# Memory products of three late batches behind U of the next batch's first step, in free columns of banks d and b; two softmax steps later

## The chip, the cores and the metric

The kernel runs on one core of one Trainium2 chip. The metric is device microseconds of one execution, lower is better. TensorE (PE in the profile) multiplies matrices into PSUM, which has eight banks of 512 fp32 columns; VectorE (DVE) and ScalarE (ACT) read PSUM and work on tiles in SBUF; SyncE (SP) issues most transfers. Each engine takes its instructions in order.

## The reference

Eight batches of eight heads, 576 positions each, head width 64, 32 memory slots per head. Then a gated layer over all 4608 rows of width 512, inner width 1536. Everything is fp32.

```python
a = exp(phi - max(phi));  a = a / (sum(a) + 1e-9)           # softmax over the memory slots
k_m = einsum('bhsm,bhsd->bhmd', a, k)                       # memory: keys and values of 32 slots
v_m = einsum('bhsm,bhsd->bhmd', a, v)
attn = softmax(q @ k_m.T / 8);  o = attn @ v_m
x = o rearranged to (4608, 512)
out = (sigmoid(x @ w_gate) * (x @ w_val)) @ w_out
```

## The kernel before

**Precision.** An fp32 product is made of three faster matmuls of a high and a low part (`_hi`, `_lo`): high by high, high by low, low by high. ScalarE rounds the high part, VectorE subtracts it from the whole (`rest`, L185). The memory products are plain fp32.

**Stages.** Batches 0 to 2 and the conversions of the weights lie in an early part, to some 287 us. The late part treats batches 3 to 7 (QUAD is 3) in 12 steps each, f = 0 to 11, one per 128 columns of the inner width. The attention's probabilities of the batch (`at`) are multiplied by U, which is v_m times the weights of two steps: in every even step `pair_u` makes the U of the next two steps in 16 fp32 matmuls (rows 64x512) into banks c and a, with weights that the transfer `ring<-wgv` has brought. A step (class `Group`) then forms its gate and value tiles by seven products p(1) to p(7) of sums of the operands, three matmuls of 128x288 each, and four out tiles of three matmuls 128x512 (`acc`). `add`, `gate`, `product_of`, `to_hi`, `to_lo` are the work on VectorE and ScalarE between a step's products and its out tiles; a step's out tiles run during the next step. In the program g is the group of this step and h the one before.

**Banks.** Four banks serve the late products: a, c, and two that change places, d in even steps and b in odd ones. Products 1, 6, 7 and 4 go into d (or b), 2 into a, 5 and 3 into c. A step's tile in d or b takes columns 0 to 287; the rest of that bank (`beside`) is free and takes the scores of the next batch in steps 2, 4, 6. Product 7 of h comes at the head of the next step, product 4 and 6 later in it: add 3 of h reads h's bank after product 7, and product 4 of h adds onto it after that.

**Order.** The order of the late loop is written out by hand; other work is hung into it at named places by `side(place)`, from a plan that `late_sides(b)` makes. In the program's order the places of a step are: "u" (behind pair_u), "m", "m3", out tiles, product 2, product 5, "E", copy p5, "act1", "B", product 4 of h, product 6, copy x, "x", "act2", out tile, "m2", product 3, "end", add 1, "B2", "act3", out tile, "Z", "load".

**Memory.** `memory(n)` is a generator whose pieces `go` calls: four transposes of the weights a and copies, then the memory products of a batch, 80 matmuls of 128 columns into 32 rows each, 40 for each half g of the heads (`kvm0` or `kvm1`, and `kvt` with `tails` for the last 64 positions), then their scaling by 1/sum (`rz`, L445 on ScalarE), four transposes of what that leaves (`row`), and copies to `kT` and `vT`. For batches 5, 6 and 7 (n > QUAD + 1) the products and the scaling lie in step f = 11 of batch n - 2, place "m", in bank a, and the transposes and copies in f = 0 of batch n - 1. The softmax of phi for those batches begins with `a_max` (L375). When a batch's memory products are done, SP may load the next batch's keys and values into the same tiles (`load_next`).

**Closing.** The two sigmoids (`gate`) of a step go at its end, or, when `close` is set, at the head of the next step behind copy s1.

Of the kernel before, what the change touches and what calls it, by code (L numbers as in the profile page):

```python
# [17 lines left out]
P = 128  # L18
B, H, S, D, M = 8, 8, 576, 64, 32
DM, DFF = 512, 1536  # L20
NG = 2
NKT = 4
NFT = DFF // P
SF = 4
# [16 lines left out]
QUAD = 3  # L41
# [63 lines left out]
def attn_moe_kernel(  # L105
# [27 lines left out]
    def bank():  # L133
        if "banks" in pools:
            return late_bank("a")
        name = next(turn_of) if spread else None
        if name is None:
            return pu.tile([P, 512], F32, name="pu_t")
        return po.tile([P, 512], F32, name=name)

    def att(shape, name, bufs=1):
        return sb.tile(shape, F32, name=name, bufs=bufs)
# [46 lines left out]
    def in_turn(do, *args, **kw):  # L189


        with ExitStack() as behind:
            if last_pe[0] is not None:
                behind.enter_context(tc.issue_after(last_pe[0].ins))
            last_pe[0] = do(*args, **kw)  # L195

    def matmul(*args, **kw):
        in_turn(nc.tensor.matmul, *args, **kw)

    def transpose(*args, **kw):  # L200
        in_turn(nc.tensor.transpose, *args, **kw)
# [196 lines left out]
    def memory(b):  # L398


        ph = loaded[b, "phi"]
        pf = ph.rearrange("p g s -> p (g s)")
        in_rows = b < QUAD or "banks" in pools
        if in_rows:
            am = [mb.tile([P, DM], F32, name="row", bufs=4) for _ in range(NG)]
            am = [t.rearrange("p (c x) -> p c x", c=SF) for t in am]
        else:
            am = att([P, 2 * S], "e")[:, : NG * SF * P]
            am = [a.rearrange("p (c x) -> p c x", c=SF) for a in (am[:, : SF * P], am[:, SF * P :])]
        for g in range(NG):  # L410
            pt = bank().rearrange("p (c x) -> p c x", c=SF)
            for c in range(SF):
                o = (g * (SF + 1) + c) * P
                transpose(pt[:, c, :], pf[:, o : o + P], ident)
            yield
            nc.scalar.copy(am[g], pt)
            yield
        pt = bank()
        transpose(pt[:, :P], pf[:, SF * P : (SF + 1) * P], ident)
        yield  # L420
        for g in range(NG):
            gs = slice(g * TAIL, (g + 1) * TAIL)
            nc.scalar.copy(tails[gs, g, :], pt[gs, :P])
        yield
        km = loaded[b, "kv"]
        kvp = bank().rearrange("p (g w d) -> p g w d", g=4, w=2)
        for g in range(NG):
            for c in range(SF + 1):
                for h in range(4):
                    hs = slice(h * M, (h + 1) * M)  # L430
                    xs = slice(h * P, (h + 1) * P)
                    if c < SF:
                        l, r = am[g][:, c, hs], km[g][:, c, xs]
                    else:
                        l, r = tails[:, g, hs], km["tail"][:, xs]
                    matmul(kvp[hs, g], l, r, start=(c == 0), stop=(c == SF))
            if g or b < QUAD:
                yield
        if in_rows:
            kb = mb.tile([P, DM], F32, name="row", bufs=4)  # L440
        else:
            kb = att([P, 2 * S], "e")[:, : NG * 4 * D]
        kb = kb.rearrange("p (g w j d) -> p g w j d", g=NG, w=2, j=2)
        for g in range(NG):
            nc.scalar.activation(  # L445
                kb[:, g],
                kvp[:, g].unsqueeze(2).broadcast_to([P, 2, 2, D]),
                AF.Copy,
                scale=loaded[b, "rz"][:, g : g + 1],
            )  # L450
        yield
        kvT = bank().rearrange("p (w g x) -> p w g x", w=2, g=NG)
        for g in range(NG):
            for w in range(2):
                transpose(kvT[:, w, g, :], kb[:, g, w].rearrange("p j d -> p (j d)"), ident)
        yield
        kvTs[b] = [keep.tile([P, NG, P], F32, name=f"{w}T", bufs=5 if w == "v" else 1) for w in "kv"]
        for w in range(2):
            nc.scalar.copy(kvTs[b][w], kvT[:, w])
            yield  # L460
# [54 lines left out]
    def s_max(b, c=None):  # L515

        e = blocks(b, c)
        w = e.shape[2]
        mx = att([P, 2, S // 32], "mx")[:, :, :w]
        nc.vector.tensor_reduce(mx, e, axis=AX.X, op=ALU.max)  # L520
        yield
        nc.vector.tensor_tensor(
            e, e, mx.unsqueeze(3).broadcast_to([P, 2, w, M]), op=ALU.subtract
        )
        yield
# [345 lines left out]
    def step(do, *args, **kw):  # L871
        with queued():
            return do(*args, **kw)
# [24 lines left out]
    now = [None, None]  # L898
# [257 lines left out]
    def late_bank(name):  # L1156
        return pools["banks"].tile([P, 512], F32, name=name)
# [72 lines left out]
    for i, (b, f, at_start, at_end) in enumerate(steps[:MAIN]):  # L1230
# [9 lines left out]
        if i in KEEP_W:  # L1240
            k = KEEP_W[i]
            w, kept_k = wg[:, 2 * k : 2 * k + 2], kept_w[k].rearrange("p (f k n) -> p f k n", f=2, k=NKT)
            move(kept_k[D:], w[D:])
            move(kept_k[:D, :, :, :P], w[:D, :, :, :P])
            for j in range(2):
                t = mb.tile([P, DM], F32, name="row", bufs=4)[:D]
                t = t.rearrange("p (k n) -> p k n", k=NKT)
# [86 lines left out]
    def late_sides(b):  # L1334

        n, m = b + 1, b + 2
        plan = {}

        def put(f, place, do, *args):
            plan.setdefault((f, place), []).append((do, args))  # L1340

        def go(x, k=1):
            for _ in range(k):
                next(memories[x])

        if n < B:
            if n > QUAD + 1:
                put(0, "m2", go, n)
                put(0, "end", go, n, 2)
            soft = [s_max(n, c) for c in range(len(ROOMFULS))]  # L1350
            norm = normalize(n)
            for c in range(len(ROOMFULS)):
                put(2 * c + 2, "u", scores, n, c)
                put(2 * c + 2, "m3", to_blocks, n, c)
                put(2 * c + 2, "Z", next, soft[c])
                put(2 * c + 3, "B", next, soft[c])
            put(6, "act3", s_exp, n, slice(0, 2 * ROOM))
            put(7, "act3", s_exp, n, 2)
            put(8, "E", next, norm)
            put(8, "Z", next, norm)  # L1360
            if m == B:
                put(9, "E", next, norm)
            put(9, "Z", cross, n)
            put(10, "B", sums_at, n, 1, 2)
            put(10, "act2", at_hi, n, "b11")
            put(10, "Z", at_lo, n, "b11")
            put(11, "m", at_hi, n, "b21")
            put(11, "E", sums_at, n, 3, 4)
            put(11, "B", at_lo, n, "b21")
            put(11, "x", at_hi, n, "t1")  # L1370
            put(11, "B2", at_lo, n, "t1")
            put(11, "act2" if m < B else "x", at_hi, n, "t2")
            put(11, "Z", at_lo, n, "t2")
        if b > QUAD:
            put(0, "act", at_hi, b, "b22")
            put(0, "act", at_hi, b, "t3")
            put(0, "E", at_lo, b, "b22")
            put(0, "B", at_lo, b, "t3")
            put(0, "act2", at_hi, b, "t4")
            put(0, "B2", at_lo, b, "t4")  # L1380
        if m < B:
            def begin_m():
                memories[m] = memory(m)

            put(2, "B", a_max, m)
            put(7, "act1", a_exp, m, (0,))
            put(7, "act2", a_exp, m, (1,))
            put(7, "Z", a_sum, m)
            put(7, "Z", begin_m)
            for f, place in ((8, "m2"), (9, "m"), (10, "m2"), (11, "m")):  # L1390
                put(f, place, go, m)
                put(f, "end" if place == "m2" else "m", go, m)
            if m + 1 < B:
                put(11, "Z", load_next, m + 1)
        if b + 1 < B:
            put(0, "load", load_q, b + 1)
        return plan
# [15 lines left out]
    for b, f in [(b, f) for b in range(QUAD, B) for f in range(NFT)]:  # L1413
        if f == 0:
            plan = late_sides(b)
# [5 lines left out]
        n = (b - QUAD) * NP + f // 2  # L1421
        odd = f % 2
        more = n + 1 < NPAIRS
        g = Group(b, f)
# [5 lines left out]
        if h:  # L1430
            step(h.add, 3)
        step(g.copy, "s1")
        if f in (2, 4, 6) and b + 1 < B:
            if b == QUAD and f == 2:
                step(part_hi, n, "s")
                step(later_lo)
            step(part_lo, n, "s")
            while gates:
                step(*gates.pop(0))
# [85 lines left out]
            step(h.to_lo)  # L1525
        side("B2")
        gates.extend([(g.gate, 0), (g.gate, 1)])
        close = f in (1, 3, 5) and b + 1 < B
        while gates and not close and not (f == 7 and b + 1 < B):
            step(*gates.pop(0))  # L1530
        side("act3")
# [85 lines left out]
```

## Time and profile before

| | |
|---|---|
| three runs | 714.0, 714.28 and 714.55 us, median 714.28 |
| the profiled execution | 713.97 us, its span 712.2 us |
| PE busy | 702.7 us, 99% of the span |
| VectorE busy | 554.1 us, 78% |
| ScalarE busy | 444.2 us, 62% |
| granted clock of TensorE | full speed in all 40 slices, mean 0.998 |

The span is what the profiler saw from the first to the last instruction; the time of the execution has 1.77 us more. Matmuls overlap in the records: rows of one product start 0.13 to 0.23 us apart and each lasts longer. The late part, in which the change lies, is 12 steps for each batch from 287 us on; f = 11 of batch 4 ends and f = 0 of batch 5 begins around 368 us.

### The profile page before, as it was taken

The page shows a single profiled execution, that of the slowest core. Times are in us where ns is not written, and L with a number is a line of the kernel's source. Part 1 is how long each engine was busy: PE and PEld are TensorE (multiplying, and loading weights), DVE is VectorE, ACT ScalarE, POOL GpSimd, SP SyncE. Part 2 cuts the span into 40 slices and gives each one's busy share as a digit, 9 for nine tenths or more (in the row PEclk, how much of TensorE's full clock was granted, in tenths as well). Part 3 has the DMA queues.
Part 4 walks back from the last instruction along what each step waited for, and adds up shares of the span by engine and source line. Part 5 has one row for each costly group of instructions (what it writes and reads, how often), then busy time and mean ns, then how long its engine had stood idle before and what let it go on. Part 6 is the DMA issues. An engine that isn't in the chain of part 4 may idle for free.

```text
span 712.2 us, 14476 instructions
## 1 busy us (share of the span) xinstructions
PE 702.7 (99%) x5623; PEld 580.2 (81%) x5623; DVE 554.1 (78%) x1108; ACT 444.2 (62%) x1033; POOL 27.9 (4%) x55
## 2 busy tenths in 40 slices
PE   8899999999999999999999999999999999999997
PEld 6666898888988888878888888888888888788886
DVE  4999998688787675588888779787797778977663
ACT  4765667544355454557877577865877667686553
POOL 0000110111100110100000000000000000000000
PEclk9999999999999999999999999999999999999999
DMA  8966768779986545641175113652213422151102
GB/s 341 410 236 247 319 191 321 284 245 278 301 241 230 185 147 199 228 143 66 60 269 201 60 61 118 228 183 82 108 64 134 159 71 75 61 175 63 61 1 74
DMA packets 36084, 123.22 MB, mean 173 GB/s; under 512 B 3952, under 2 KB 11376, under 8 KB 28848
## 3 DMA queue, kind: packets, MB, share of 16 engines
q1 hardware_dynamic: 31296, 106.71, 42.7%
q0 software_dynamic: 4560, 15.47, 6.1%
q8 instruction: 44, 0.72, 0.4%
q14 instruction: 24, 0.20, 0.1%
q10 hardware_dynamic: 160, 0.13, 0.1%
HBM read 96.73 MB, written 25.56 MB: 172 GB/s over the span
## 4 chain that ended last, share of the span: by engine, by line
PE 92%; DVE 4%; DMA 2%; ACT 1%; issue 1%; SPq 0%; DVEq 0%; ACTq 0%
PE acc L195 38%; PE pu_t L195 21%; PE c L195 11%; PE a L195 8%; PE b L195 7%; PE d L195 7%; DMA q<-in_qT_dram 1%; DMA ph<-in_phiT_dram 1%; DVE wg L286 0%; DVE nmx L375 0%; DVE e L513 0%; DVE u_lo L185 0%; DVE row L772 0%; ACT ph L170 0%; DVE left L286 0%
## 5 line engine op out<-in xcount | busy, mean ns | idle before, releaser
L195 PE MATMUL acc<-wo_hi,g_hi 128*128 128x512 f32 x372 | 151.4, 407 | 0.0
L195 PE MATMUL acc<-wo_hi,g_lo 128*128 128x512 f32 x372 | 147.1, 395 | 0.4 <-DVE g_lo L185 0.4
L195 PE MATMUL acc<-wo_lo,g_hi 128*128 128x512 f32 x372 | 146.5, 394 | 0.0
L195 PE MATMUL pu_t<-at,u_hi 128*128 128x320 f32 (+1 forms) x560 | 116.5, 304 | 0.8 <-DVE at L185 0.8
L195 PEld LDWEIGHTS pu_t<-at,u_hi 128*128 128x128 f32 x560 | 92.1, 188 | 8.7 <-issue 1.9
L195 PEld LDWEIGHTS acc<-wo_hi,g_hi 128*128 128x128 f32 x372 | 69.8, 188 | 29.6 <-issue 10.6
L195 PEld LDWEIGHTS acc<-wo_hi,g_lo 128*128 128x128 f32 x372 | 69.8, 188 | 18.1 <-DVE g_lo L185 1.1
L195 PE MATMUL pu_t<-at,u_lo 128*128 128x256 f32 (+1 forms) x264 | 77.5, 294 | 0.0
L195 PEld LDWEIGHTS acc<-wo_lo,g_hi 128*128 128x128 f32 x372 | 70.0, 188 | 5.4
L1198 ACT COPY c_p<-c 128x288 f32<-128x288 f32 x60 | 24.0, 399 | 61.3 <-PE c L195 60.6
L170 ACT ACTIVATE sg<-pu_t 128x256 f32<-128x256 f32 (+1 forms) x70 | 28.6, 412 | 48.3 <-PE pu_t L195 40.9
L1202 DVE TENSOR_TENSOR z<-a,c_s 128x288 f32<-128x288 f32 x60 | 27.1, 452 | 32.0 <-PE a L195 31.9
L722 ACT CAST g_hi<-sg 128x256 fp32r<-128x256 f32 x66 | 26.4, 406 | 38.2 <-DVE sg L712 37.2
L712 DVE TENSOR_TENSOR sg<-pu_t,sg 128x320 f32<-128x320 f32 (+1 forms) x69 | 30.9, 453 | 24.1 <-ACT sg L170 14.0
L195 PEld LDWEIGHTS pu_t<-at,u_lo 128*128 128x128 f32 x264 | 49.6, 188 | 0.0
L170 ACT ACTIVATE z<-z 128x288 f32<-128x288 f32 x120 | 47.9, 442 | 1.5 <-DVE z L1202 0.8
L1214 ACT CAST g_hi<-z 128x512 fp32r<-128x512 f32 x60 | 37.4, 623 | 17.9 <-DVE z L1209 17.8
L1202 DVE TENSOR_TENSOR z<-c,c_x 128x288 f32<-128x288 f32 x60 | 27.3, 455 | 27.3 <-PE c L195 24.5
L185 DVE TENSOR_TENSOR g_lo<-z,g_hi 128x512 fp32r<-128x512 f32 x60 | 41.0, 684 | 2.3 <-ACT g_hi L1214 2.3
L195 PE MATMUL a<-ring,vT 64*32 64x512 f32 x232 | 31.4, 601 | 0.0
L195 PE MATMUL c<-ring,vT 64*32 64x512 f32 x232 | 31.4, 601 | 0.0
L1209 DVE TENSOR_TENSOR z<-z 128x288 f32<-128x288 f32 x60 | 27.0, 450 | 5.4 <-ACT z L170 0.7
(242 smaller groups left out, 1631.3 us busy)
## 6 DMA issues: line engine op xcount, KB each, us to landing
ring<-wgv SPq DMA_DIRECT2D x30, 1024.0 KB, 4.9
kvm<-in_kvm_dram SPq DMA_DIRECT2D x14, 1024.0 KB, 8.6
at<-at SPq DMA_DIRECT2D x18, 576.0 KB, 7.5
q<-in_qT_dram SPq DMA_DIRECT2D x16, 512.0 KB, 5.2
part<-row POOLq DMA_DIRECT2D x24, 256.0 KB, 5.6
row<-part SPq DMA_DIRECT2D x24, 256.0 KB, 4.0
words<-in_wo_dram SPq DMA_DIRECT2D x8, 512.0 KB, 8.3
words<-in_wgv_dram SPq DMA_DIRECT2D x4, 1024.0 KB, 5.9
```

The costliest lines, as they stand in the source:

```text
L170: last_act[0] = nc.scalar.activation(*args, **kw)
L185: return nc.vector.tensor_tensor(lo, x, hi.bitcast(F32), op=ALU.subtract)
L195: last_pe[0] = do(*args, **kw)
L712: last_prod[0] = nc.vector.tensor_tensor(prod, ps[1][:, :n], sg[:, :n], op=ALU.mult)
L722: nc.scalar.copy(hi, prod[:, : 2 * P])
L1198: copy(getattr(self, name), self.c if name == "p5" else self.d)
L1202: nc.vector.tensor_tensor(self.z[:, i], x, y, op=ALU.add)
L1209: nc.vector.tensor_tensor(self.z[:, 2 + i], x, self.z[:, i], op=ALU.mult)
L1214: nc.scalar.copy(self.g[0], self.z[:, 2:4, : 2 * P])
```

## The change

Four things. First, for batches 5, 6 and 7 (`aside`) the memory products go from f = 11, "m", to the next batch's f = 0, "u", that is behind pair_u. They don't go into bank a but into columns 288 and up of banks that steps hold: half 0 into the bank of h (b, from f = 11), half 1 into that of g (d), without clearing the bank at the start. Their scaling goes to f = 0, "act1". Second, `close` is set in f = 11 too. Third, `a_max` of batch 5 goes from f = 2 of batch 3 to f = 4. Fourth, in batch 6 the last batch's `cross` (the transpose of probabilities, L969) goes from f = 9, "Z", to f = 10, "m3", and two of its sums from "B" to "B2".

```diff
+        aside = b > QUAD + 1
+        kvp = [unit.beside[:, :P] for unit in now] if aside else bank().rearrange("p (g x) -> p g x", g=4)
+        kvp = [kvp[g] if aside else kvp[:, g] for g in range(NG)]
...
-                    matmul(kvp[hs, g], l, r, start=(c == 0), stop=(c == SF))
+                    matmul(
+                        kvp[g][hs], l, r, start=c == 0 and not aside, stop=c == SF, skip_group_check=aside,
+                    )
...
             if n > QUAD + 1:
+                put(0, "u", go, n)
+                put(0, "act1", go, n)
                 put(0, "m2", go, n)
                 put(0, "end", go, n, 2)
...
-            put(9, "Z", cross, n)
-            put(10, "B", sums_at, n, 1, 2)
+            put(*((9, "Z") if m < B else (10, "m3")), cross, n)
+            put(10, "B" if m < B else "B2", sums_at, n, 1, 2)
...
-            put(2, "B", a_max, m)
+            put(4 if b == QUAD else 2, "B", a_max, m)
...
-            for f, place in ((8, "m2"), (9, "m"), (10, "m2"), (11, "m")):
+            for f, place in ((8, "m2"), (9, "m"), (10, "m2")):
...
-        if f in (2, 4, 6) and b + 1 < B:
+        if f in (2, 4, 6) and b + 1 < B or f == 0 and QUAD < b < B - 1:
...
-        close = f in (1, 3, 5) and b + 1 < B
+        close = f in (1, 3, 5) and b + 1 < B or f == NFT - 1 and b + 2 < B
```

On PE, in f = 0 of batch 5, the memory products (`b<-kvm0`, `d<-kvm1`, and `kvt` with `tails`) stand in the changed order behind the last matmul of U (`a<-ring`):

```order
L195 MATMUL a_4568<-ring_4417,vT_3544 32x512
L195 MATMUL b_4485<-kvm0_3589,row_4303 32x128 [waits DVE_49]
L195 MATMUL b_4485<-kvm0_3589,row_4303 32x128 x15
L195 MATMUL b_4485<-kvt_3587,tails_83 32x128 x4
L195 MATMUL d_4558<-kvm1_3591,row_4304 32x128 [waits Activation_49]
L195 MATMUL d_4558<-kvm1_3591,row_4304 32x128 x15
L195 MATMUL d_4558<-kvt_3587,tails_83 32x128 x4
L195 MATMUL acc0_3775<-wo2_hi_2397,g2_hi_4524 128x512
```

Before, the first out tile (`acc0`) came there, and the memory products stood in f = 11 in bank a; the wait for DVE in the second row is for add 3 of h (`z<-b,c_p5`), which reads bank b.

On PE in the same step, from product 5 (`c`) through product 4 of h (`b`) to product 6 (`d`), first of the kernel before:

```order
L195 MATMUL c_4644<-at_3317,s_lo_4416 128x288 [waits DVE_49]
L195 MATMUL b_4485<-at_3319,u_hi_4252 128x288 [waits DVE_49]
L195 MATMUL b_4485<-at_3320,u_hi_4252 128x288
L195 MATMUL b_4485<-at_3319,u_lo_4253 128x288
L195 MATMUL d_4605<-at_3319,s_hi_4415 128x288
```

and of the change:

```order
L195 MATMUL c_4640<-at_3317,s_lo_4416 128x288 [waits DVE_49]
L195 MATMUL b_4485<-at_3319,u_hi_4252 128x288 [waits Activation_49]
L195 MATMUL b_4485<-at_3320,u_hi_4252 128x288
L195 MATMUL b_4485<-at_3319,u_lo_4253 128x288
L195 MATMUL d_4558<-at_3319,s_hi_4415 128x288 [waits Activation_49]
```

The matmuls stand as they stood; the first of product 4 and the first of product 6 wait for ScalarE, where product 4 waited for VectorE and product 6 for nothing.

On ScalarE in the same step, from the casts of the probabilities (`at`) through the copies of product 5 and of bank d (`c_p5`, `c_x`), first of the kernel before:

```order
L1000 CAST at_3319<-q_4390 128x288
L1000 CAST at_3317<-q_4390 128x288
L1198 COPY c_p5_4599<-c_4644 128x288 [waits PE_49,Activation_49]
L1198 COPY c_x_4600<-d_4605 128x288 [waits DVE_49,PE_49]
L1214 CAST g2_hi_4660<-z_4481 128x512 [waits DVE_49]
```

and of the change:

```order
L1005 CAST at_3317<-q_4390 128x288
L1203 COPY c_p5_4552<-c_4640 128x288 [waits PE_49,Activation_49]
L450 ACTIVATE row_4647<-b_4485,rz_4226 128x256 [waits DMASW7_49,DMAHW1_49,DMASW1_49,DVE_49]
L450 ACTIVATE row_4647<-d_4558,rz_4226 128x256
L1203 COPY c_x_4553<-d_4558 128x288 [waits PE_49]
```

The two scalings of the memory (`row<-b,rz` and `row<-d,rz`) stand between the two copies; before they stood in f = 11 and read bank a.

## Rows read from the trace of the kernel before

**Rows 1.** The page: busy us, share of the span and instructions of each engine.

```profile
PE 702.7 (99%) x5623; PEld 580.2 (81%) x5623; DVE 554.1 (78%) x1108; ACT 444.2 (62%) x1033; POOL 27.9 (4%) x55
```

**Rows 2.** Timeline, PE in f = 11 of batch 4: start, us, engine, line, operation, out<-in.

```profile
360.81 0.43 PE L195 MATMUL b<-at,u_hi 128*128 128x288 f32 x2
...
361.30 1.08 PE L195 MATMUL a<-kvm,row 128*32 128x128 f32 x32
...
363.62 0.50 PE L195 MATMUL acc<-wo_hi,g_hi 128*128 128x512 f32 x1
...
363.96 0.39 PE L195 MATMUL acc<-wo_lo,g_hi 128*128 128x512 f32 x1
```

**Rows 3.** Timeline, PE in f = 0 of batch 5.

```profile
369.82 0.59 PE L195 MATMUL c<-ring,vT 64*32 64x512 f32 x1
...
370.39 0.50 PE L195 MATMUL acc<-wo_hi,g_hi 128*128 128x512 f32 x1
...
372.29 0.42 PE L195 MATMUL c<-at,s_hi 128*128 128x288 f32 x2
...
372.69 0.42 PE L195 MATMUL b<-at,u_hi 128*128 128x288 f32 x2
```

**Rows 4.** Timeline, DVE from f = 11 to f = 0 there.

```profile
365.77 0.46 DVE L1202 TENSOR_TENSOR z<-a,c_s 128x288 f32<-128x288 f32 x1 [1.75 <-PE a L195]
...
367.11 0.45 DVE L1209 TENSOR_TENSOR z<-d,z 128x288 f32<-128x288 f32 x1
...
370.35 0.45 DVE L185 TENSOR_TENSOR at<-q,at 128x288 fp32r<-128x288 f32 x1
...
370.72 0.45 DVE L1202 TENSOR_TENSOR z<-b,c_p 128x288 f32<-128x288 f32 x1
```

**Rows 5.** Timeline, DVE in f = 11 of batch 6, which has no memory products.

```profile
620.13 0.45 DVE L1209 TENSOR_TENSOR z<-d,z 128x288 f32<-128x288 f32 x1
...
621.27 0.69 DVE L185 TENSOR_TENSOR g_lo<-z,g_hi 128x512 fp32r<-128x512 f32 x1 [0.32 <-ACT g_hi L1214]
...
621.88 0.45 DVE L185 TENSOR_TENSOR at<-q,at 128x288 fp32r<-128x288 f32 x1
```

**Rows 6.** Timeline, ACT from f = 11 to f = 0 of batch 5.

```profile
363.76 0.84 ACT L445 ACTIVATE row<-a,rz 128x256 f32<-128x256 f32 x2 [0.83 <-PE a L195]
...
372.94 0.40 ACT L1198 COPY c_p<-c 128x288 f32<-128x288 f32 x1 [0.64 <-PE c L195]
```

**Rows 7.** Line 445, late batches: shortest, median and longest in ns, first and last start.

```profile
L445 ACT ACTIVATE row<-a,rz x6: 466/472/476, 363.8 to 534.2; 128x256 f32<-128x256 f32 x6
```

**Rows 8.** Timeline, PE and DVE in f = 2 of batch 3.

```profile
305.14 0.43 PE L195 MATMUL c<-at,u_hi 128*128 128x288 f32 x2
...
306.57 1.34 DVE L375 TENSOR_REDUCE nmx<-ph 128x2 f32<-128x1152 f32 x1
...
310.09 0.50 PE L195 MATMUL acc<-wo_hi,g_lo 128*128 128x512 f32 x1 [0.36 <-DVE g_lo L185]
...
310.82 0.42 PE L195 MATMUL c<-at,u_hi 128*128 128x288 f32 x2
```

**Rows 9.** Timeline, PE and DVE in f = 2 of batch 4.

```profile
385.43 0.42 PE L195 MATMUL c<-at,u_hi 128*128 128x288 f32 x2
...
386.00 1.34 DVE L375 TENSOR_REDUCE nmx<-ph 128x2 f32<-128x1152 f32 x1
...
390.28 0.42 PE L195 MATMUL c<-at,u_hi 128*128 128x288 f32 x2
```

**Rows 10.** Timeline, PE in f = 10 of batch 6.

```profile
611.59 0.43 PE L195 MATMUL c<-at,u_hi 128*128 128x288 f32 x2
...
616.69 0.43 PE L195 MATMUL c<-at,u_hi 128*128 128x288 f32 x2
```

**Rows 11.** DMA issues from 360 to 384 us: KB each, median us from issue to landing.

```profile
kvm<-in_kvm_dram SPq DMA_DIRECT2D x2, 1024.0 KB, 6.6
```

**Rows 12.** Timeline, PE: U of f = 2 in batch 5.

```profile
382.14 0.61 PE L195 MATMUL c<-ring,vT 64*32 64x512 f32 x1
```

More of the change, by code (lines that the diff above doesn't have):

```diff
@@ L425, in memory @@
         km = loaded[b, "kv"]
-        kvp = bank().rearrange("p (g w d) -> p g w d", g=4, w=2)
+        aside = b > QUAD + 1
+        kvp = [unit.beside[:, :P] for unit in now] if aside else bank().rearrange("p (g x) -> p g x", g=4)
+        kvp = [kvp[g] if aside else kvp[:, g] for g in range(NG)]
+        kvp = [t.rearrange("p (w d) -> p w d", w=2) for t in kvp]
         for g in range(NG):
@@ L446, in memory @@
                 kb[:, g],
-                kvp[:, g].unsqueeze(2).broadcast_to([P, 2, 2, D]),
+                kvp[g].unsqueeze(2).broadcast_to([P, 2, 2, D]),
                 AF.Copy,
```

## Prediction

> **What bounds the kernel now.** I read the page's busy shares first: TensorE (PE in the rows) is at work for 702.7 of the span's 712.2 us [rows 1], and its granted clock is at full speed in all 40 slices. So a microsecond comes off only where PE has less to issue or stops waiting, and a microsecond goes on wherever PE is made to wait; ScalarE (ACT) and VectorE (DVE) count only where PE stands in line behind them. Next I read the timeline of the two steps that the change touches, f = 11 of batch 4 and f = 0 of batch 5 (batches 6 and 7 repeat it). In f = 11 the memory products lie between product 1 and the out tiles without a hole [rows 2], and in f = 0 PE goes from U to the out tiles and from product 5 to product 4 without one [rows 3]. In these two steps there is thus no stall to win; what the change can bring there is the small cost of switching shapes, and what it can lose is a new wait.
>
> **The move of the memory products.** The matmuls stay the same, 80 of them (40 per half). *Taken out of f = 11:* product 1 starts at 360.81 and a product occupies PE for 0.40 (372.29 to 372.69 in rows 3), so the first out matmul could start at 361.21; it starts at 363.62, and it is 0.50 long where the next is 0.39 [rows 2]. That is 2.41 + 0.11 = 2.52 us out. *Put into f = 0:* from the first memory product to the out tile it is 363.62 - 361.30 = 2.32 [rows 2]; the step from U's second half to what follows, 370.39 - 369.82 = 0.57 [rows 3], is paid already, with whichever block follows. So -0.2 per batch. I keep 0 and -0.35 as bounds, since no row shows this block right behind U.
>
> **First new wait: half 0 behind add 3.** In the changed order half 0 is written into bank b (the first order fence), and PE waits there for DVE: b still holds product 7 of the step before, which add 3 reads. When does add 3 end? Measure all on the old time axis, with PE 2.52 earlier after f = 11's place "m". Half 0 would be due at 369.82 - 2.52 + 0.57 = 367.87. On DVE, add 0 now idles 1.75 for PE [rows 4]; that idle goes, but no more than that, for DVE itself is full from there on. So the product with gate 0 starts at 367.11 - 1.75 = 365.36. From it to the g_lo of the same step it is 621.27 - 620.13 = 1.14 where DVE runs without PE's memory block, and 0.61 from g_lo to the next remainder [rows 5]; two more starts at 0.37 (370.35 to 370.72) and add 3's own 0.45 follow [rows 4]. That is 365.36 + 1.14 + 0.61 + 0.37 + 0.37 + 0.45 = 368.30, or some 368.25 if DVE catches up its little. PE waits from 367.87 to there: **+0.4** per batch, bounds 0.2 and 0.55. Behind the waiting matmul on PE stand both halves, the out tiles, and products 2 and 5. Half 1 goes into bank d and waits for ACT's copy of that bank; the copy needs product 1 alone, which lies ahead of U, and is done before half 0 is.
>
> **Second new wait: product 4 behind the scale.** Product 4 accumulates into bank b's first 288 columns, and half 0 now lies in b's other columns until ACT has scaled it. In the second order fence product 4 waits for ACT where it waited for DVE before; the third shows where the scale stands on ACT: right behind the copy of product 5. But product 5 is the product directly before product 4 on PE. So PE must finish 5, ACT must copy it, then scale half 0, and only then may 4 start. With S the start of product 5: the copy starts at S + 0.65 (372.94 - 372.29) and lasts 0.40 [rows 3, 6]. A scale lasts 0.472 [rows 7], and two of them 0.84 together [rows 6], so neighbours on ACT overlap by 0.10. The scale of half 0 ends at S + 0.65 + 0.40 - 0.10 + 0.47 = S + 1.42; product 4 started at S + 0.40 before [rows 3]. That is 1.02 later; with a first matmul 0.11 slower after the hole, as behind the memory block [rows 2], it is **+1.1** per batch, bounds 0.9 and 1.2. Nothing covers it: between 5 and 4 the list gives PE no other work. Product 6 then needs the scale of half 1, which ends 0.37 after the first; 6 stands 0.40 behind 4, so it waits for nothing more. Behind 4 everything moves along: the product with gate 1, g_hi, g_lo, the transposes of the scaled memory (these get more room, the scale being earlier beside them), and the next step.
>
> The Trainium skill, *PSUM — Partial Sum Buffer*, section "PSUM bank collisions raise a hardware error", says that no two engines may access one bank within the same 32 partitions at the same time, disjoint columns included, and that software must put a dependency there. This speaks against the change: columns that are free are not a bank that is free. By that page the two waits stand, as in the sum; were columns independent, the sum would lose them, which is the second rival. No row of before shows two engines inside one late bank at a time, and none shows the contrary.
>
> Per batch: -0.2 + 0.4 + 1.1 = +1.3; three batches **+3.9** (bounds 2.3 and 5.2, from the ends of all three at once).
>
> **The maximum.** In batch 3's f = 2 the reduction of 1.34 us stands in DVE's line, g_lo comes late, and the third out matmul waits 0.36 for it [rows 8]. The step from product 5 to product 5 is 310.82 - 305.14 = 5.68; the same step of batch 4, also with a reduction in it, has 390.28 - 385.43 = 4.85 and no stall [rows 8, 9]. So **-0.83** when it leaves f = 2. At f = 4 it meets a step like batch 4's and costs 0 by that row; the upper bound is what it cost before, 0.83.
>
> **The turned probabilities (batch 6).** The transpose, in f = 9's place "Z", makes DVE late in f = 10: that step is 616.69 - 611.59 = 5.10 [rows 10] where 4.85 is the clean length [rows 9], so at most -0.25. One step later, DVE has the same work to do before f = 11's products: **-0.1**, bounds -0.25 and 0.
>
> **Closing the gates later** (ACT's two sigmoids and a DVE remainder move from the end of f = 11 into f = 0): ACT idled 0.64 before its copy of product 5 [rows 6], and the memory products put 2.32 more between; two sigmoids over as many columns as that copy (0.40) fit in that. 0.
>
> **Loads.** The loads for the next batch's keys and values now wait for the later products, and the ring load for U of f = 2 stands behind them on SP. One of the two large ones takes 6.6 us to land [rows 11], the ring load is as large as one, and the three stand one behind the other: 9.9 in all if the two large ones shared those 6.6 us, 13.2 if not; I take the middle, 11.6. Room, from the end of the products (370.39 on the old axis) to U of f = 2 at 382.14 [rows 3, 12]: 11.75, and the second wait adds 1.1. So 0, and up to 1 per batch, in two batches only, since for batch 7 nothing is loaded.
>
> Sum: 3.9 - 0.83 - 0.1 = +2.95 us (rounded 3.0). The profiled execution took 713.97, its span 712.2, with 1.77 outside; the new span comes to 715.15 and this execution to 716.9. The median of the three runs is 714.28, 0.31 above the profiled one; on it the forecast is **717.2 us**.
>
> **Rivals.** *A load is late* (chance 0.09): the chain of loads overruns its room by 0.5 in two batches, 717.2 + 1.0 = 718.2. For it: room and length are nearly equal. Against: the wait for the scale lengthens the room. *The first wait isn't there* (0.12): DVE catches up in f = 11, where nothing else holds it, and PE waits for the scale alone: 717.2 - 1.2 = 716.0. For it: 0.4 is a small difference of two long chains. Against: DVE's work there is counted from rows. *The bank waits cost nothing* (0.06), the other side: the scale of half 0 is over when product 4 comes up, because ACT gets to it early, or columns of a bank stand alone. Then 3 x -0.2 - 0.83 - 0.1 = -1.5, 712.8 us. It decides when the waits are under 0.5 per batch in sum, at which the time is that of before ((0.83 + 0.1) / 3 + 0.2). For it: the products of all other rows in f = 0 lose nothing. Against: on ACT's list the scale stands behind a copy that cannot start before product 5 ends, and PE has nothing in between.
>
> **How the numbers follow.** The forecast has 0.73, with its own range 716.3 to 718.0 (each term about half of the way to its bound, three times over). The range 715.6 to 718.3 takes in the one-wait case with its spread and the late load's middle; left out are the case without waits and the worst of the loads. A difference of 0.2%, 1.43 us, is about what a measurement of this kernel can tell from no change. Faster by that means under 712.85: two thirds of the last rival, 0.04. Within it, up to 715.71: the rest of it and the low tail of the one-wait case, 0.08. Slower: 0.88.
>
> **What would show it.** In the changed profile product 4 of f = 0 in batches 5 to 7 should begin some 1.45 after product 5, with an idle time put down to ACT's scale; the first memory product some 0.4 late, put down to DVE's add 3; out tiles of f = 11 directly behind product 1; batch 3's f = 2 in 4.85. The prediction is wrong if product 4 follows product 5 at 0.40, if the first out matmul after f = 0's U is not displaced by more than 2.4, or if U of f = 2 waits for its ring load.

## The result, and the profile after

| | median | lowest to highest | runs |
|---|---|---|---|
| before | 714.18 us | 713.97 to 714.55 | 6 |
| changed | 719.01 us | 717.18 to 720.21 | 6 |

The ratio is 1.0064, with a 95% interval of 1.0054 to 1.0074: the change costs 4.6 us, or 0.6% (the two medians themselves are 4.8 apart). The forecast was 717.2, its range ended at 718.3. The direction was right, the size too small. The changed kernel's six runs differ by 3 us and the six of before by 0.6; over the 27 runs of before that went with later experiments it was 2.9 too (713.68 to 716.61), so the spread alone says little.

Batches are counted below as the late loop counts them (its `b`). Counted so, the rows from 360 to 373 us are f = 11 of batch 3 and f = 0 of batch 4: two steps after product 5 at 372.29 [rows 3] comes f = 2 of batch 4 at 385.43 [rows 9]. The headings of [rows 2], [rows 3], [rows 4], [rows 6] and [rows 12], the text on the site around 368 us and the prediction put them one batch too high; [rows 5] and [rows 8] to [rows 10] are counted right. The three sites of the move are f = 11 of batches 3, 4 and 5, each with f = 0 of the next batch. No sum changes by this.

The profiled execution is the slowest of the six, 720.21 us with a span of 718.4 (before 713.97 and 712.2), so it shows the loss at its largest. The page's shares hardly move (compare [rows 1]); the view of what waits for what, PE's rows, says more. Its columns are the engine, tile and line that waited, what for, us in total, times, and the longest:

```profile
PE b L195 <- ACT row L450: 2.8, 3, 0.9
PE b L195 <- DMA q<-in_qT_dram: 2.7, 2, 2.0
...
PE b L195 <- DVE z L1207: 0.9, 3, 0.3
```

None of the three rows has a counterpart in the kernel before. The first and the third are the two bank waits of the forecast, three times each. The second, scores waiting for a load of q, isn't in it.

PE in the timeline of the changed kernel, from f = 11 of batch 3 into f = 0 of batch 4 (rows 2 and 3 are the same places before):

```profile
359.96 0.29 PE L195 MATMUL b<-at,u_lo 128*128 128x288 f32 x1
...
360.09 0.40 PE L195 MATMUL acc<-wo_hi,g_hi 128*128 128x512 f32 x1
...
366.20 0.59 PE L195 MATMUL c<-ring,vT 64*32 64x512 f32 x1
...
367.14 1.08 PE L195 MATMUL b<-kvm,row 128*32 128x128 f32 x32 [0.30 <-DVE z L1207]
...
369.46 0.50 PE L195 MATMUL acc<-wo_hi,g_hi 128*128 128x512 f32 x1
...
371.36 0.43 PE L195 MATMUL c<-at,s_hi 128*128 128x288 f32 x2
...
372.84 0.53 PE L195 MATMUL b<-at,u_hi 128*128 128x288 f32 x2 [0.92 <-ACT row L450]
```

The out tile of f = 11 now follows product 1 at once. From U's second half to the memory products it is 0.94, where 0.57 stood ahead of the out tile [rows 3]: 0.37 for add 3. The block itself takes 2.32 as before, and product 4 starts 1.48 after product 5, which was 0.40.

What they wait for, on DVE and ACT of the same execution:

```profile
364.15 0.45 DVE L1214 TENSOR_TENSOR z<-d,z 128x288 f32<-128x288 f32 x1
...
365.29 0.69 DVE L185 TENSOR_TENSOR g_lo<-z,g_hi 128x512 fp32r<-128x512 f32 x1 [0.33 <-ACT g_hi L1219]
...
365.90 0.82 DVE L185 TENSOR_TENSOR at<-q,at 128x288 fp32r<-128x288 f32 x2
...
366.64 0.45 DVE L1207 TENSOR_TENSOR z<-b,c_p 128x288 f32<-128x288 f32 x1
...
372.01 0.40 ACT L1203 COPY c_p<-c 128x288 f32<-128x288 f32 x1 [2.95 <-PE c L195]
...
372.31 0.48 ACT L450 ACTIVATE row<-b,rz 128x256 f32<-128x256 f32 x1
372.67 0.48 ACT L450 ACTIVATE row<-d,rz 128x256 f32<-128x256 f32 x1
```

Add 3 ends at 367.09 and the first memory product starts at 367.14. ACT idles for 2.95 us, and for most of that time the products that it is to scale lie ready; then come the copy of product 5, the scale of half 0 to 372.79, and product 4 at 372.84.

Step by step, from the start of one product 5 to the start of the next, in the profiled executions (us; batch of the later product for the second column):

| kernel | f = 10 of batch 3 | f = 11, into batch 4 | f = 0 of 4 | f = 1 of 4 | f = 1 of 5 | f = 2 of 3 | f = 10 + 11 of 6 |
|---|---|---|---|---|---|---|---|
| before | 8.18 | 6.79 | 5.29 | 7.85 | 7.84 | 5.68 | 5.10 + 7.47 |
| changed | 5.68 | 9.48 | 6.49 | 8.79 | 10.11 | 4.87 | 4.88 + 7.83 |

The product 5 that begins "f = 10" is f = 10's, so f = 11's memory block lies in that column. The other two sites of the move repeat the first three columns within 0.05. Thus a site costs -2.50 + 2.69 + 1.20 = 1.39. The two columns "f = 1" reach into U and the scores of f = 2: +0.94 and +2.27, which is the load of q. In f = 1 of batch 6, where no loads of keys and values stand ahead of q, nothing is lost (7.86 in both).

SP's queue at the first site and the first score matmul of f = 2 in batches 4 and 5, in the changed kernel:

```profile
369.59 0.33 SPq L181 DMA_DIRECT2D kvt<-in_kvt_dram  x1
369.97 0.90 SPq L181 DMA_DIRECT2D kvm<-in_kvm_dram  x2
370.92 0.43 SPq L181 DMA_DIRECT2D ring<-wgv  x1
376.99 1.28 SPq L181 DMA_DIRECT2D q<-in_qT_dram  x3
...
384.20 0.35 PE L195 MATMUL b<-q,kT 64*32 64x224 f32 x1 [0.71 <-DMA q<-in_qT_dram]
...
472.92 0.35 PE L195 MATMUL b<-q,kT 64*32 64x224 f32 x1 [2.02 <-DMA q<-in_qT_dram]
```

In the kernel before, the first of these two matmuls came earlier and without a wait:

```profile
383.02 0.35 PE L195 MATMUL b<-q,kT 64*32 64x224 f32 x1
```

The loads' time from issue to landing (KB each, median us), of the changed kernel from 369 to 385 us:

```profile
kvm<-in_kvm_dram SPq DMA_DIRECT2D x2, 1024.0 KB, 7.1
ring<-wgv SPq DMA_DIRECT2D x2, 1024.0 KB, 9.1
q<-in_qT_dram SPq DMA_DIRECT2D x2, 512.0 KB, 7.6
```

and of the kernel before, where the same loads begin 6 us earlier, in the window of [rows 11]:

```profile
ring<-wgv SPq DMA_DIRECT2D x2, 1024.0 KB, 5.1
q<-in_qT_dram SPq DMA_DIRECT2D x2, 512.0 KB, 4.5
```

q is issued when its tile comes free, at 376.99 against 376.73 before, so it isn't late in starting. But the keys and values, 2.25 MB, start at 369.59 and no more at 363.75; the ring load stands behind them, and q behind both. It lands after 7.6 us where it took 4.5. The scores of f = 2, right behind U, are the first to need it.

### The profile page after: what moved, and what is told of

It reads as the page before. It is cut to its first block, busy times and chain, and to the rows that moved or that the text cites. A ratio compares the mean times of both kernels' runs of the same rounds, so it can differ in the third digit from the quotient of the medians.

```text
span 718.4 us, 14472 instructions
## 1 busy us (share of the span) xinstructions
PE 702.1 (98%) x5623; PEld 579.8 (81%) x5623; DVE 553.2 (77%) x1108; ACT 443.4 (62%) x1033; POOL 27.8 (4%) x55
## 4 chain that ended last, share of the span: by engine, by line
PE 86%; DVE 8%; DMA 3%; ACT 1%; issue 1%; SPq 0%; DVEq 0%; ACTq 0%
PE acc L195 36%; PE pu_t L195 20%; PE c L195 9%; PE a L195 7%; PE b L195 7%; PE d L195 7%; DMA q<-in_qT_dram 2%; DMA ph<-in_phiT_dram 1%; DVE at L185 1%; DVE wg L286 1%; DVE z L1207 1%; DVE q L980 1%; DVE g_lo L185 1%; DVE nmx L375 0%; DVE s_lo L185 0%
```

## The experiments

Ten kernels, all with their own runs of the kernel before on the same chip (median 714.2 to 714.4).

**Loads of keys and values behind q** (`loads_later`).

```diff
-                put(11, "Z", load_next, m + 1)
+                put(11, "Z", load_phi, m + 1)
...
             put(0, "load", load_q, b + 1)
+        if b > QUAD and m < B:
+            put(1, "load", load_kv, m)
```

> The changed kernel (719.0 us) with one thing moved: the loads of the next batch's keys and values go from the end of f = 11 to f = 1 of the next batch, so that on SP they stand behind the load of q and not ahead of it; phi's load stays. Theory 1 (the scores of f = 2 wait for a load of q that shares its time with these loads, 0.7 and 2.0 us in the profile): those two waits vanish, the time falls to 717.3 to 717.8, and the runs lie within some 0.6 us of each other instead of 3. Rival (the loss is on the engines, and the late load only shows it): 718.6 to 719.2.

718.43 us (718.28 to 719.42), ratio 1.0057 [1.0045, 1.0070]. f = 1 of batches 4 and 5 are 7.88 and 7.84: the wait for q is gone. A new one has come, once, in f = 3 of batch 5 (8.97 where 8.20 is usual), at U of f = 4:

```profile
482.95 0.59 PE L195 MATMUL c<-ring,vT 64*32 64x512 f32 x1 [0.72 <-DMA ring<-wgv]
```

On SP the moved loads now stood just ahead of that ring load (470.66 and 471.71). The theory holds for q. Its numbers don't: the time lies above the expected range and the runs spread over 1.1 us, not 0.6. The new wait of 0.7 is what the trace shows for it.

**The same at the end of f = 2** (`loads_f2`).

```diff
-            put(1, "load", load_kv, m)
+            put(2, "load", load_kv, m)
```

> The changed kernel with the loads of keys and values one step later still, at the end of f = 2, behind the ring load that U of f = 4 needs (at f = 1 they stood ahead of it, and U of f = 4 waited 0.7 for it). Theory 1 (the late loads are a matter of order on SP and of shared time): no wait for a load is left between f = 0 and f = 4 of batches 5 and 6; the two bank waits stay: late part 3.5 above that of before, 717.2 to 717.9. Rival (loads are late whatever their order): a wait for a load shows elsewhere, 718.4 as with f = 1.

717.9 us (717.7 to 718.98), ratio 1.0051 [1.0039, 1.0064]. No wait for a load is left in the late part: f = 1 has 7.88 and 7.84, f = 3 8.19 and 8.20. So the engines' own loss is 717.9 - 714.4 = 3.5, and the late q adds 719.0 - 717.9 = 1.1 in the median (3.2 in the profiled execution). The intervals of the two ratios overlap, so the size of 1.1 is uncertain; that the wait was there and is gone, the traces show. The table's sum without q agrees: 3 x 1.39 - 0.81 + 0.14 = 3.5.

**The scale ahead of the copy** (`scale_early`).

```diff
-                put(0, "act1", go, n)
+                put(0, "E", go, n)
```

> The changed kernel with the scaling of the memory in f = 0 moved from behind the copy of product 5 to just ahead of it on ScalarE; nothing else. Theory 1 (product 4 waits for the scale only because the scale stands behind that copy): product 4 follows product 5 at 0.40 again in all three batches, which is 1.15 us each. In batch 7's case that stays won; in the two others the room for the load of q shrinks by as much, so some of it goes to that wait: 716.5 to 717.9. Rival A (the load is no bound): 715.5. Rival B (the bank's sharing itself holds product 4, not the order on ScalarE): 719.0.

715.64 us (714.01 to 718.13), ratio 1.0015 [1.0002, 1.0028]: 3.4 us less than the changed kernel. Timeline, ACT and PE in f = 0 of batch 4:

```profile
369.80 0.49 ACT L450 ACTIVATE row<-b,rz 128x256 f32<-128x256 f32 x1
...
370.45 0.47 ACT L450 ACTIVATE row<-d,rz 128x256 f32<-128x256 f32 x1 [0.16 <-PE d L195]
...
372.22 0.42 PE L195 MATMUL c<-at,s_hi 128*128 128x288 f32 x2
...
372.62 0.42 PE L195 MATMUL b<-at,u_hi 128*128 128x288 f32 x2
...
372.87 0.40 ACT L1203 COPY c_p<-c 128x288 f32<-128x288 f32 x1 [1.94 <-PE c L195]
```

Product 4 follows product 5 at 0.40 again, and f = 0 takes 5.29 to 5.31 at all three sites. The scale runs in time in which ACT was idle. This refutes rival B: bank b is shared as before, and product 4 waits no more. The median stands near rival A's number, but not for rival A's reason. Without any late load it would be some 717.9 (`loads_f2`) less 3 x 1.19, or 714.3, so late loads still cost about 1.3 in the median, much as in the changed kernel. In the profiled execution f = 1 of batch 5 takes 9.36 where 7.84 is usual: U of f = 2 waits 0.53 for its ring load there, and the scores behind it 0.67 for q.

**A remainder behind add 3** (`add3_early`).

```diff
-            put(11, "Z", at_lo, n, "t2")
+            if n == B - 1:
+                put(11, "Z", at_lo, n, "t2")
...
+                put(0, "u", at_lo, b, "t2")
                 put(0, "u", go, n)
```

> The changed kernel with one remainder of the probabilities (VectorE, 0.45 us) moved from ahead of add 3 to behind it, in f = 0 of batches 4, 5 and 6. Theory 1 (the memory products wait for add 3): their wait of 0.30 in the profile goes to about 0 in all three batches; 0.3 is won in the last, and in the two others the late load of q may take it back: 718.1 to 718.8. Rival (VectorE is late for another reason, or the wait is the switch of shapes): the wait stays, 719.0.

717.9 us (716.62 to 718.71), ratio 1.0047 [1.0034, 1.0059], 1.1 less than the changed kernel. The step across f = 11 falls from 9.48 to 9.13, 9.11 and 9.12. DVE and PE in f = 0 of batch 4:

```profile
367.56 0.45 DVE L185 TENSOR_TENSOR at<-q,at 128x288 fp32r<-128x288 f32 x1
367.93 0.45 DVE L1207 TENSOR_TENSOR z<-b,c_p 128x288 f32<-128x288 f32 x1
...
368.44 1.08 PE L195 MATMUL b<-kvm,row 128*32 128x128 f32 x32
```

PE has no idle time in front of the memory products. 3 x 0.36 = 1.1, so by the medians q took nothing back, and the time is a little under the expected range. In the profiled execution the scores still wait for q once, 0.89 in batch 5.

**Without the closing** (`no_close`), on the version with the loads at f = 2.

```diff
-        if f in (2, 4, 6) and b + 1 < B or f == 0 and QUAD < b < B - 1:
+        if f in (2, 4, 6) and b + 1 < B:
...
-        close = f in (1, 3, 5) and b + 1 < B or f == NFT - 1 and b + 2 < B
+        close = f in (1, 3, 5) and b + 1 < B
```

> The kernel with the loads at the end of f = 2 (717.9 us), without the closing in f = 11: the sigmoids and one remainder of 768 columns stand again at the end of f = 11, and that remainder (VectorE, 0.94) ahead of add 3. Theory 1 (the memory products wait for add 3, so what stands ahead of it on VectorE costs its whole length): the wait grows from 0.30 to some 1.2 in all three batches, 720.3 to 720.9. Rival (closing is without effect, as the prediction's term of 0 said): 717.7 to 718.1.

721.07 us (720.97 to 721.7), ratio 1.0093 [1.0079, 1.0106]: 3.2 more. The steps across f = 11 are 10.59, 10.57 and 10.61, 1.1 longer each.

```profile
367.27 0.96 DVE L185 TENSOR_TENSOR s_lo<-s_raw,s_hi 128x768 fp32r<-128x768 f32 x1
368.14 0.45 DVE L185 TENSOR_TENSOR at<-q,at 128x288 fp32r<-128x288 f32 x1
368.51 0.45 DVE L1207 TENSOR_TENSOR z<-b,c_p 128x288 f32<-128x288 f32 x1
...
369.02 1.08 PE L195 MATMUL b<-kvm,row 128*32 128x128 f32 x32 [1.42 <-DVE z L1207]
```

The remainder of 0.96 stands ahead of add 3, and PE waits 1.42 for it instead of 0.30. That is 0.2 a batch more than the remainder's own length; the edit also moves the two sigmoids on ACT, and what the 0.2 is stays open. Closing is what keeps the first wait small.

**All three mended** (`all_three`): the edits of `scale_early`, `add3_early` and `loads_later` together.

> The changed kernel with all three: the scale ahead of the copy, the remainder behind add 3, the loads of keys and values behind the load of q. Theory 1 (these three waits are all that the move of the memory products costs): the products then gain 0.1 to 0.2 in each batch for one switch of shapes less, the maximum 0.8: 712.6 to 713.3, below the kernel before (714.2). Rival (products in shared banks, or closing later, cost something by themselves): 714.2 or more.

714.11 us (713.08 to 715.29), ratio 0.9996 [0.9987, 1.0005]. The bank waits are gone (9.10 and 5.31 in the first site's columns), but the ring wait of `loads_later` comes here as well: f = 3 of batch 5 takes 9.37, 1.17 too long. That accounts for the miss (714.1 against a middle of 712.95); the trace shows nothing of the rival's reason.

**Mended, loads at f = 2, turned probabilities as before** (`best`).

```diff
-            put(1, "load", load_kv, m)
+            put(2, "load", load_kv, m)
...
-            put(*((9, "Z") if m < B else (10, "m3")), cross, n)
-            put(10, "B" if m < B else "B2", sums_at, n, 1, 2)
+            put(9, "Z", cross, n)
+            put(10, "B", sums_at, n, 1, 2)
```

> The changed kernel with the scale ahead of the copy, the remainder behind add 3, the loads at the end of f = 2, and the last batch's transpose and sums back where they were before. Theory 1: each batch's move now gains 0.17 by the steps measured (-2.49 + 2.31 + 0.01), the maximum 0.81, the transposes no longer lose 0.14: 714.2 - 0.5 - 0.8 = 712.9 (712.5 to 713.3). Rival (a load is late here too): 713.8 to 714.3.

713.22 us (712.9 to 714.8), ratio 0.9985 [0.9976, 0.9994]. The site, on PE:

```profile
367.29 1.08 PE L195 MATMUL b<-kvm,row 128*32 128x128 f32 x32
...
369.61 0.51 PE L195 MATMUL acc<-wo_hi,g_hi 128*128 128x512 f32 x1
...
371.51 0.42 PE L195 MATMUL c<-at,s_hi 128*128 128x288 f32 x2
371.91 0.42 PE L195 MATMUL b<-at,u_hi 128*128 128x288 f32 x2
```

Its three columns are 5.69, 9.11 and 5.30, in sum 20.10 against 20.26 before: 0.16 a batch for the switch of shapes that is saved. f = 10 of batch 6 took 5.45 here, 0.35 more than before.

**The same with the turned probabilities as changed** (`best_turned`).

> The changed kernel with the scale ahead of the copy, the remainder behind add 3 and the loads at the end of f = 2, and with the turned probabilities as in the change. In the version with these put back, f = 10 of batch 6 took 5.45 where the kernel before has 5.10. Theory 1 (behind the moved products f = 10 and f = 11 take 4.88 + 7.84 with this part, 5.45 + 7.46 without): 0.2 better than that version, 713.0, which is under 714.2 by more than the noise of either. Rival (5.45 was one execution's): equal to it within 0.2, 713.2.

713.35 us (712.37 to 714.44), ratio 0.9987 [0.9978, 0.9996]. f = 10 and f = 11 of batch 6 are 4.88 and 7.83, as expected, but between the two medians there is no difference that these runs can tell. No other kernel has the combination in which f = 10 took 5.45, so whether that was one execution's stays open. Both versions stand level with the maximum alone (`amax_only`, next): 713.2 and 713.35 against 713.49, which these runs can't tell apart.

**The maximum alone** (`amax_only`), on the kernel before.

```diff
-            put(2, "B", a_max, m)
+            put(4 if b == QUAD else 2, "B", a_max, m)
```

> The kernel before with one part of the change alone: the maximum of batch 5 at f = 4 of batch 3. Theory 1: the step f = 2 falls from 5.68 to 4.87, f = 4 stays 4.88: 713.4. Rival (the wait comes back later, at f = 4, or in a wait for a load): 714.2.

713.49 us (712.92 to 714.73), ratio 0.9986 [0.9977, 0.9995]. PE, the starts of product 5 in f = 2, 3, 4 and 5 of batch 3:

```profile
304.98 0.42 PE L195 MATMUL c<-at,u_hi 128*128 128x288 f32 x2
...
309.85 0.42 PE L195 MATMUL c<-at,u_hi 128*128 128x288 f32 x2
...
318.03 0.43 PE L195 MATMUL c<-at,s_hi 128*128 128x288 f32 x2
...
322.90 0.43 PE L195 MATMUL c<-at,s_hi 128*128 128x288 f32 x2
```

f = 2 takes 4.87 (5.68 in [rows 8]), and f = 4, which now holds the reduction, 4.87 too.

**The turned probabilities alone** (`cross_only`), on the kernel before.

```diff
-            put(9, "Z", cross, n)
-            put(10, "B", sums_at, n, 1, 2)
+            put(*((9, "Z") if m < B else (10, "m3")), cross, n)
+            put(10, "B" if m < B else "B2", sums_at, n, 1, 2)
```

> The kernel before with another part alone: the last batch's transposed probabilities and two sums later. Theory 1 (read from the changed kernel): f = 10 of batch 6 goes from 5.10 to 4.88 and f = 11 from 7.47 to 7.83, so 714.3, nothing that this comparison can tell. Rival (f = 11's 0.36 comes from the move of the memory products, not from this part): f = 11 stays 7.47, 714.0.

714.22 us (713.8 to 714.89), ratio 0.9999 [0.9990, 1.0008]. Product 5 of f = 10 and f = 11 of batch 6 and of f = 0 of batch 7:

```profile
611.70 0.43 PE L195 MATMUL c<-at,u_hi 128*128 128x288 f32 x2
...
616.58 0.43 PE L195 MATMUL c<-at,u_hi 128*128 128x288 f32 x2
...
624.42 0.49 PE L195 MATMUL c<-at,s_hi 128*128 128x288 f32 x2
```

4.88 and 7.84: f = 10 wins 0.22, f = 11 loses 0.37, without any memory product moved. The loss is at the head of batch 7's f = 0, where product 1 writes bank d, which DVE still reads at the end of f = 11:

```profile
620.40 0.45 DVE L1209 TENSOR_TENSOR z<-d,z 128x288 f32<-128x288 f32 x1
...
620.91 0.53 PE L195 MATMUL d<-at,s_hi 128*128 128x288 f32 x2
```

DVE's read ends at 620.85. It began at 620.13 before [rows 5], 0.27 earlier (though product 5 of f = 11 came 0.11 later there), and PE didn't have to wait for it.

## Why the prediction was right and where it failed

**The two bank waits** were right in place and close in size. The move out of f = 11 won 2.50 (2.52 said); back in with the wait for add 3 it cost 2.69 (2.32 + 0.4 said); the wait for the scale cost 1.20 (1.1 said). A site cost 1.39, the forecast said 1.3. Two edits that touch one wait each took away 1.19 and 0.36 a site, so the cause is shown, not only read: it is what stands ahead of the release on ACT and on DVE. The last rival, bank waits that cost nothing, is out for this order; with the scale and the remainder moved it describes `best`.

**The step that failed is "Loads".** The text priced the ring load for U of f = 2 against its room and put 0, "up to 1 per batch". The sum of that chain was good: from the first load of keys to the ring load's landing it took 11.8 and 12.5 us at the two sites (11.6 said), and the ring load was in time, by 1.1 and 0.3. The load of q behind it wasn't. The room was taken to U, and the scores right behind U, which need q, weren't looked at. q starts no later than before, and so looked untouched; but in the kernel before its 4.5 us, from 376.73, ended some 2 us before the scores (383.02), and with the loads ahead of it 6 us later it took 3 us longer, 5 at the second site. Without the wait for q the change gives 717.9 (`loads_f2`), inside the forecast's range. The text's three signs of being wrong ask for product 4, the out matmul and the ring load; none of them came true, since none asks for q. The rival "a load is late" had the mechanism in kind with 0.09 and a price of 1.0; the median loss is 1.1, and in single executions up to 3.2.

The Trainium skill, *DMA: Bandwidth & Descriptors*, section "Queues, rings and completion order", says that the loads issued by SP run through one row of rings, each consumed in order, but also that a later one may complete before an earlier one. By that page q stands in line behind the ring load and the keys, with no rule on which lands first. The trace agrees with the first and shows no such overtaking: all of SP's 196 transfers landed in the order of issue, the ring load of 370.92 after 10.4 us and the first part of q, issued at 376.99, after 7.1. A load of 512 KB took 7.6 us in place of 4.5, and 4.2 in `loads_f2`:

```profile
q<-in_qT_dram SPq DMA_DIRECT2D x2, 512.0 KB, 4.2
ring<-wgv SPq DMA_DIRECT2D x1, 1024.0 KB, 5.8
```

Whether q was late by its place in the queue or by sharing the transfer with the loads ahead isn't separated: `loads_later` and `loads_f2` change both. The same load issued by another engine would help to tell; it wasn't run.

**The maximum** won 0.81 in its step (0.83 said) and cost nothing at f = 4. **The turned probabilities** were mis-signed: -0.1 said, +0.14 measured. What f = 10 won, 0.22, was less than what DVE, late at the end of f = 11, cost product 1 of the next step, 0.37; the text looked at f = 11's products and not at that bank. **Closing** at 0 was right only as part of the whole: the sum for add 3 already had the remainder behind it. By itself, in the moved order, it is worth 1.1 a batch.

Put together: forecast +2.95 (its terms add up to 2.97); the sites' 0.27 and the probabilities' 0.24 make it 3.5, and q's 1.1 makes it 4.6.

## What to carry to other kernels

Free columns in a bank that is still in use were a queue here, not a place: whatever reads them had to be done before the bank's next writer, so the reader has to stand, on its own engine, ahead of whatever waits for the product just before that writer. When a buffer's last use moves later, follow every load on that queue to its first reader, those that start no later included. Look for a move's loss in its neighbours' order: three edits to the order took the changed kernel from 719.0 to 713.35 (`best_turned`). That isn't yet a gain of the move, since the maximum alone gives 713.49; by the steps the mended move wins 0.16 a site. So measure each part of a change by itself before crediting the whole.

## What the runs showed of the hardware

A load of 512 KB issued at the same time took 4.5 us or, with 3.25 MB issued 6 to 7 us ahead of it on the same queue, 7.6 us. The wait that follows was 0.71 and 2.02 at two like places of one execution, and 1.1 in sum by the medians of `loads_f2` and the changed kernel, whose intervals overlap.
